# Eight rows for q and k, a permuted key order in PSUM, and a constant column for 1e-9 in a forgetting-attention and SwiGLU kernel

## The chip, the cores and the metric

The kernel runs on one core of one Trainium2 chip. The metric is device time in microseconds, and the median of three runs is the number that counts. The engines are named as in the profile: PE (TensorE, the matrix engine; PEld is its weight load), DVE (VectorE), ACT (ScalarE), POOL (GpSimd) and SP (SyncE, which here only issues DMAs). SBUF is the on-chip memory with 128 partitions, and PSUM is the small memory into which TensorE writes.

## The reference

Attention with a forget gate per position, then a SwiGLU feed-forward block over the heads put side by side. All inputs are float32.

```python
B, H, S, D = 8, 8, 576, 64
scores = (1 / sqrt(D)) * q @ k.T                       # per batch and head
cum    = cumsum(log(clip(f, 1e-4, 1)), axis=-1)
decay  = cum[..., :, None] - cum[..., None, :]
scores = where(causal, -1e9, scores + decay)           # causal: strictly above the diagonal
scores = scores - max(scores)
attn   = exp(scores)
attn   = attn / (sum(attn) + 1e-9)
x      = (attn @ v), heads side by side                # 4608 tokens x 512
g      = x @ w_gate                                    # 512 x 1536
out    = (g * sigmoid(g) * (x @ w_val)) @ w_out        # 1536 x 512
```

The term of the row in `decay` is the same for a whole row and cancels in the softmax, so only the column's `cum` matters.

## The kernel before, in words

**The planner.** The kernel lists some thousand operations, each with the engines that may run it, a price in ns on each, what it reads and writes, and a priority. A greedy list scheduler, `Plan.order` (L54), walks through them: it picks the operation and engine that can start first by those prices, gives it a buffer out of its pool, and so fixes the order on every engine. The buffers of a pool go out in a fixed turn. Each engine then runs its list in order. A changed price therefore changes the order of everything behind it. `SPARE` (L205) is a handicap that keeps some operations off ACT and DVE unless these are clearly earlier.

**The attention.** Work goes by pairs of heads: 32 pairs, four per batch (`p`). A pair's 576 queries are nine blocks of 64; a block of both heads fills the 128 output partitions. Blocks 0 to 3 are group 0 and blocks 4 to 8 group 1. For a pair:

- `load_pair` (L319) loads q and k with SP's queue: k as 96 partitions of 6 rows, q as 72 partitions of 8 rows (`ROWS`, L182). It also loads `cb`, the cumulated gates, spread over the partitions.
- `prepare` (L336) casts both to bfloat16 (L345 to L351; POOL, in the start also ACT or DVE) and transposes them on TensorE into a PSUM bank (L363): six transposes of 96 columns for k, eight of 72 for q. In the bank the positions then stand in the order (row within the partition, partition). The copy out of PSUM (L377 on ACT, L379 on DVE) reads them one by one in the order of the sequence: one copy of 128 partitions into `kt`, and two of 64 partitions into `qz`, which holds each head's queries in its own half, with zeros in the other.
- `scores` (L384) multiplies a block's queries with its keys (L398) and adds the mask of the diagonal block with an identity as weights (L402), with scores in PSUM with a minus sign. One DVE instruction (L414) then adds `cb` into `t` and takes the minimum of each row, and ACT takes the exponential with that minimum as bias and sums each row into `ls` (L428).
- `normalize` (L434) adds 1e-9 to `ls` in place (L437) and takes the reciprocal (L439), both on DVE; POOL (in the first eight pairs also ACT) multiplies the rows and packs them into `pk` as bfloat16 (L456). The packed weights are transposed by TensorE in the first eight pairs (L480, copied out at L485), and by DMA later.
- `weighted` multiplies with v (L506) and `spread` copies the result into `xT` (L530 on DVE or ACT), which feeds the feed-forward part.

**The feed-forward part.** Tiles of 256 or 512 tokens; per unit `gate` (L572) does the two products (L587), tanh on ACT into `th` (L593), and two DVE products (L595, L598) into `hh`; `project` multiplies with `w_out` (L612). Three PSUM banks (`gv`) serve the two products and the transposes. The feed-forward part of earlier tokens is threaded in between the attention of later ones; after about 345 us it is alone.

**The start.** The gates are clipped, taken the logarithm of, and cumulated by a DVE scan (L302), whose first input is a tile of ones.

Of the kernel before, what the change touches and what calls it, by code (L numbers as in the profile page):

```python
# [14 lines left out]
BIG = 1.0e9  # L15
# [142 lines left out]
def kernel(  # L158
# [23 lines left out]
    ROWS = {"k": (96, 6), "q": (72, 8)}  # L182
    scale = 1.0 / (D ** 0.5)
    assert NB * QB == S and D == 64 and all(a * b == S for a, b in ROWS.values())
# [39 lines left out]
    ident = sb.tile([P, P], BF16)  # L224
    maskf = sb.tile([P, QB], F32)
# [6 lines left out]

    bufs("qf", [P, 2, ROWS["q"][1] * D], F32, 2)
    bufs("kf", [P, 2, ROWS["k"][1] * D], F32, 2)
    bufs("qb", [P, ROWS["q"][1], 2, D], BF16, 2)
    bufs("kb", [P, ROWS["k"][1], 2, D], BF16, 2)
# [8 lines left out]
    bufs("ls", [P, NB], F32, 6)  # L245
# [5 lines left out]
    bufs("th", [P, 512], F32, 3)  # L251
# [10 lines left out]
    for h in range(2):  # L262
        nc.gpsimd.affine_select(
            out=maskf[64 * h:64 * h + 64, :], in_=maskf[64 * h:64 * h + 64, :],
            compare_op=ALU.is_ge, fill=BIG, base=0, pattern=[[-1, QB]], channel_multiplier=1,
        )
# [7 lines left out]
    setup({"POOL": 200}, lambda e: nc.gpsimd.tensor_copy(mask, maskf), ["mask"], -150)  # L274
    for n, qz in enumerate(pl.pools["qz"]):
        setup({"DVE": 800, "POOL": 1100}, lambda e, qz=qz: (eng[e].memset(qz[0:64, :, 1, :], 0.0),
                                                            eng[e].memset(qz[64:128, :, 0, :], 0.0)),
              [("z", "qz", n)], -95 if n == 0 else first[n] - 1.5)
    for i in range(0, NB, 2):
        for n, e_ in enumerate(pl.pools[f"e{i}"]):  # L280
            setup({"POOL": 100}, lambda e, e_=e_, i=i: nc.gpsimd.memset(e_[:, QB * (i + 1):], 0.0),
                  [("z", f"e{i}", n)], -80 if i < 4 else 1)
# [5 lines left out]
    ones = sb.tile([P, S], F32)  # L288
    pl.op({"POOL": 520}, lambda e: nc.gpsimd.memset(ones, 1.0), (), ["ones"], -200)
# [4 lines left out]
    def gates(key, parts, np_, prio):  # L294
        x = lambda: pl.buf(key)[0:np_, :]
        for n, (a, z, src) in enumerate(parts):
            loads["f", key, n] = pl.op({"SP": 600}, lambda e, a=a, z=z, src=src: nc.sync.dma_start(out=pl.buf(key)[a:z, :], in_=src),
                                       (), [(key, 0)] + [key] * (n == 0), prio + n * .01, dma=500)
        pl.op({"DVE": 460}, lambda e: nc.vector.tensor_scalar(x(), x(), 1.0e-4, 1.0, op0=ALU.max, op1=ALU.min),
              [(key, 0)], [(key, 1)], prio, holds=[key])  # L300
        pl.op({"ACT": 690}, lambda e: nc.scalar.activation(x(), x(), AF.Ln), [(key, 1)], [(key, 2)], prio, holds=[key])
        pl.op({"DVE": 1350}, lambda e: nc.vector.tensor_tensor_scan(x(), ones[0:np_, :], x(), 0.0, ALU.mult, ALU.add),  # L302
              [(key, 2), "ones"], [(key, 3)], prio, holds=[key])
# [15 lines left out]
    def load_pair(p):  # L319
        b, hp = divmod(p, NPB)  # L320
        s = first[p]
        for name, src, pr in (("k", k, 0), ("q", q, .1)):
            pl.key((name + "f", p), name + "f")
            loads[name, p] = pl.op({"SP": 620} if p else {"ACT": 620}, lambda e, name=name, src=src: (nc.scalar if e == "ACT" else nc.sync).dma_start(
                out=pl.buf((name + "f", p))[0:ROWS[name][0], :, :],
                in_=src[b, 2 * hp:2 * hp + 2].rearrange("h (p r) d -> p h (r d)", r=ROWS[name][1])),
                (), [(name + "f", p)], (-99 + 3 * p if p < NPB else s) + pr, dma=1130 if name == "k" else 980, after=[sums[p - 3, 0 if p - 3 >= NPB else 1]] if p >= NPB else [])
        if p >= NDIRECT:
            pl.key(("cb", p), "cb")
            for h in range(2):  # L330
                loads["cb", p, h] = pl.op({"SP": 600}, lambda e, h=h: nc.sync.dma_start(
                    out=pl.buf(("cb", p))[64 * h:64 * h + 64, :],
                    in_=cum_dram[2 * p + h:2 * p + h + 1, :].to_broadcast((64, S))),
                    ["cum_dram"], [("cb", p), (("cb", p), 3)], -98.5 + 3 * p if p < NPB else s + .2, dma=560)

    def prepare(p):  # L336
        s = first[p]
        for name in ("k", "q"):
            fk, bk = (name + "f", p), (name + "b", p)
            KR, KC = ROWS[name]  # L340
            pl.key(bk, name + "b")

            def cast(e, name=name, fk=fk, bk=bk, KR=KR):
                src = pl.buf(fk)[0:KR, :, :].rearrange("p h (r d) -> p r h d", d=D)
                dst = pl.buf(bk)[0:KR, :, :, :]  # L345
                if e == "ACT":
                    nc.scalar.activation(dst, src, AF.Copy, scale=-scale if name == "q" else 1.0)
                elif name == "q":
                    eng[e].tensor_scalar(dst, src, -scale, 1.0, op0=ALU.mult, op1=ALU.mult)  # L349
                else:  # L350
                    eng[e].tensor_copy(dst, src)  # L351
            engs = {"POOL": 850}
            if p < NPB:
                engs = {"POOL": 850, "ACT": 850, "DVE": 500} if name == "k" else {"POOL": 1050, "ACT": 1050, "DVE": 680}
# [5 lines left out]
            def transpose(e, bk=bk, tk=tk, KR=KR, KC=KC):  # L360
                src = pl.buf(bk).rearrange("p r h d -> p r (h d)")
                for j in range(KC):
                    nc.tensor.transpose(half(tk)[:, KR * j:KR * j + KR], src[0:KR, j, :], ident[0:KR, 0:KR])  # L363
            pl.op({"PE": KC * (KR / 2.4 + 2.5)}, transpose, [bk], [tk], s - 1, lat=200)
# [3 lines left out]
            for a, z, h in halves:  # L368
                def evac(e, a=a, z=z, h=h, tk=tk, ok=ok, KC=KC):
                    if h is None:  # L370
                        src = half(tk)[a:z, 0:S].rearrange("r (j p) -> r p j", j=KC)
                        dst = pl.buf(ok)[a:z, :].rearrange("r (p j) -> r p j", j=KC)
                    else:
                        src = half(tk)[a:z, 0:S].rearrange("r (j i p) -> r i p j", j=KC, i=NB)
                        dst = pl.buf(ok)[a:z, :, h, :].rearrange("r i (p j) -> r i p j", j=KC)
                    if e == "ACT":
                        nc.scalar.copy(dst, src)  # L377
                    else:
                        nc.vector.tensor_copy(dst, src)  # L379
                pl.op({"ACT": 600, "DVE": 680}, evac, [tk] + ([("z", "qz", p)] if h is not None and p < 5 else []), [ok], s - .9)  # L380
# [4 lines left out]
    def scores(p, g):  # L385
# [3 lines left out]
        for n, bank in enumerate(BANKS[g]):  # L389
# [4 lines left out]
            def mult(e, bank=bank, sk=sk):  # L394
                sp, kt, qz, o = pl.buf(sk), pl.buf(("kt", p)), pl.buf(("qz", p)), 0
                for i, a, z in bank:
                    last = z == QB * (i + 1)
                    nc.tensor.matmul(sp[:, o:o + z - a], qz[:, i, :, :].rearrange("p h r -> p (h r)"), kt[:, a:z],  # L398
                                     start=True, stop=not last)
                    o += z - a  # L400
                    if last:
                        nc.tensor.matmul(sp[:, o - QB:o], ident, mask, start=False, stop=True)  # L402
            cols = [z - a for _, a, z in bank] + [64 for i, a, z in bank if z == QB * (i + 1)]
            pl.op({"PE": mm(*cols)}, mult, [("kt", p), ("qz", p), "mask"], [sk], pr, lat=220)
            o = 0
            for i, a, z in bank:
# [5 lines left out]
                def add(e, i=i, a=a, z=z, o=o, sk=sk, tk=tk, last=last):  # L412
                    tm = pl.buf(("tm", p, g))
                    nc.vector.tensor_tensor_reduce(  # L414
                        out=pl.buf(tk)[:, a:z], in0=pl.buf(sk)[:, o:o + z - a], in1=pl.buf(("cb", p))[:, a:z], scale=1.0,
# [6 lines left out]
                if last:  # L422
# [3 lines left out]
                    def exp(e, i=i, tk=tk, ek=ek):  # L426
# [3 lines left out]
                                             accum_out=pl.buf(("ls", p, g))[:, i:i + 1])  # L430
# [3 lines left out]
    def normalize(p, g):  # L434
        s = at[p, g]
        ls = lambda: pl.buf(("ls", p, g))[:, LO[g]:HI[g] + 1]
        pl.op({"DVE": 90}, lambda e: nc.vector.tensor_scalar(ls(), ls(), 1.0e-9, None, op0=ALU.add),  # L437
              [("ls", p, g)], [("l1", p, g)], s, lat=120)
        pl.op({"DVE": 95}, lambda e: nc.vector.reciprocal(ls(), ls()), [("l1", p, g), ("ls", p, g)], [("l2", p, g)], s, lat=100)  # L439
# [3 lines left out]
        for i in range(HI[g], LO[g] - 1, -1):  # L443
            m = i // 2 + 1
            parts = [(0, m)] if (g, i) != (1, 8) else [(0, 4), (4, 5)]
            for c0, c1 in parts:
                def norm(e, i=i, c0=c0, c1=c1):
# [4 lines left out]
                    r = pl.buf(("ls", p, g))[:, i:i + 1]  # L452
# [6 lines left out]
                if p < FREE:  # L459
                    engs["ACT"] = L * .833 + 150  # L460
                o = pl.op(engs, norm,
                      [("e", p, i), ("l2", p, g), ("ls", p, g)] + [("z", f"e{i}", n) for n in range(2) if p == 0 and i % 2 == 0],
# [50 lines left out]
    def spread(p, g):  # L513
# [5 lines left out]
        for a, z in ((0, cut), (cut, w)):  # L519
# [3 lines left out]
            def evac(e, a=a, z=z):  # L523
                x0 = (t0 + a * QB) % NRING
                dst = xT[:, hp, x0:x0 + QB * (z - a)].rearrange("p (i r) -> p i r", r=QB)
                x = w - z
                src = pl.buf(xk)[:, QB * x:QB * (x + z - a)].rearrange("p (i r) -> p i r", r=QB)
                full = [list(d) for d in src.ap]
                src = bass.AP(src.tensor, src.offset + QB * (z - a - 1), [full[0], [-QB, z - a], full[2]])
# [181 lines left out]
```

## Time and profile before

| | |
|---|---|
| median of 3 runs | 439.18 us (438.22 to 440.01) |
| profiled execution | 437.54 us, span 435.8 us, mean granted TensorE clock 0.99 |
| PE busy | 405.7 us (93%) |
| DVE busy | 354.0 us (81%) |
| ACT busy | 296.7 us (68%) |
| POOL busy | 250.3 us (57%) |

The costliest groups of DVE, ACT and POOL (busy us, mean ns of one) that the change touches:

| line, engine | what | count | busy | mean |
|---|---|---|---|---|
| L414 DVE | subtraction and row minimum, all widths | 288 + 32 | 138.9 | |
| L379 DVE | copies of `kt` and `qz` out of PSUM | 53 | 39.7 | 750 |
| L377 ACT | the same on ACT | 43 | 27.0 | 627 |
| L351 POOL | cast of k | 31 | 25.4 | 821 |
| L349 POOL | cast of q | 31 | 33.0 | 1063 |
| L437 DVE | the addition of 1e-9 | 64 | 18.9 | 295 |
| L439 DVE | the reciprocal | 64 | 11.3 | 176 |
| L530 DVE, ACT | copy of the result into `xT` | 64 | 26.7 | |

The profile shows one execution. "Busy" is the time in which an engine had an instruction at work; matmuls are pipelined, so that a matmul's own duration (379 ns for 512 columns) is longer than the distance of two starts (216 ns). The chain of waits is the path of work that ended last, followed back from the end. A time on an engine matters where that engine is on this path or holds up one that is.

### The profile page before, as it was taken

The page shows a single profiled execution, that of the slowest core. Times are in us where ns is not written, and L with a number is a line of the kernel's source. Part 1 is how long each engine was busy: PE and PEld are TensorE (multiplying, and loading weights), DVE is VectorE, ACT ScalarE, POOL GpSimd, SP SyncE. Part 2 cuts the span into 40 slices and gives each one's busy share as a digit, 9 for nine tenths or more (in the row PEclk, how much of TensorE's full clock was granted, in tenths as well). Part 3 has the DMA queues.
Part 4 walks back from the last instruction along what each step waited for, and adds up shares of the span by engine and source line. Part 5 has one row for each costly group of instructions (what it writes and reads, how often), then busy time and mean ns, then how long its engine had stood idle before and what let it go on. Part 6 is the DMA issues. An engine that isn't in the chain of part 4 may idle for free.

```text
span 435.8 us, 9810 instructions
## 1 busy us (share of the span) xinstructions
PE 405.7 (93%) x3192; PEld 231.6 (53%) x3192; DVE 354.0 (81%) x1109; ACT 296.7 (68%) x824; POOL 250.3 (57%) x443
## 2 busy tenths in 40 slices
PE   2588999998899899999999999999999999999996
PEld 1445877755355455554554555555555444457672
DVE  7788799779999889999999999899999665365340
ACT  6887899979669767987766778787777633232321
POOL 6679828738957867787568677838973600000000
PEclk9996999999999999999999999999999999999999
DMA  7999899547869999999999999999984740010111
GB/s 201 213 193 233 173 204 212 149 125 202 191 149 221 218 224 207 203 231 217 219 204 228 208 206 222 201 197 218 208 160 99 119 106 26 24 50 24 50 50 72
DMA packets 143955, 72.50 MB, mean 166 GB/s; under 512 B 118560, under 2 KB 130592, under 8 KB 143904
## 3 DMA queue, kind: packets, MB, share of 16 engines
q1 hardware_dynamic: 137732, 66.57, 71.2%
q0 software_dynamic: 5808, 4.72, 7.3%
q10 hardware_dynamic: 364, 0.59, 0.5%
q8 instruction: 25, 0.41, 0.4%
q14 instruction: 26, 0.21, 0.2%
HBM read 47.33 MB, written 9.58 MB: 131 GB/s over the span
## 4 chain that ended last, share of the span: by engine, by line
PE 71%; DVE 13%; ACT 7%; issue 3%; DMA 2%; POOL 2%; SPq 1%; DVEq 0%; ACTq 0%
PE gv L587 35%; PE op L612 15%; PE sp L398 8%; PE tx L506 5%; DVE t L414 4%; PE tx L363 3%; ACT e L428 2%; PE gv L480 2%; PE gv L612 2%; ACT qz L377 2%; DVE qz L379 2%; DVE hh L598 2%; DMA qf<-in_q_dram 2%; DVE th L595 1%; ACT eo L428 1%
## 5 line engine op out<-in xcount | busy, mean ns | idle before, releaser
L414 DVE CUSTOM_DVE_ANT_0 t<-sp,cb 128x512 f32<-128x512 f32 (+7 forms) x288 | 130.2, 473 | 6.9 <-PE sp L402 3.1
L456 POOL TENSOR_SCALAR pk<-e,ls 128x128 bf16<-128x128 f32 (+3 forms) x184 | 98.1, 537 | 58.4 <-DVE tm L414 21.2
L587 PE MATMUL gv<-xT,wg 128*128 128x512 bf16 (+1 forms) x528 | 112.0, 342 | 0.0
L587 PE MATMUL gv<-xT,wv 128*128 128x512 bf16 (+1 forms) x528 | 111.2, 340 | 0.0
L428 ACT ACTIVATE e<-t,tm 128x448 f32<-128x448 f32 (+4 forms) x160 | 88.5, 554 | 26.4 <-DVE tm L414 26.0
L595 DVE SCALAR_TENSOR_TENSOR th<-th,gv 128x512 f32<-128x512 f32 x108 | 73.7, 683 | 37.4 <-ACT th L593 37.0
L593 ACT ACTIVATE th<-gv 128x512 f32<-128x512 f32 x108 | 63.7, 590 | 58.0 <-PE gv L587 57.1
L612 PE MATMUL op<-wo,hh 128*128 128x512 bf16 x396 | 100.6, 379 | 1.5 <-DVE ot L624 1.4
L398 PE MATMUL sp<-kt,qz 128*128 128x448 bf16 (+4 forms) x320 | 75.1, 301 | 10.2 <-DVE tm L414 8.5
L598 DVE TENSOR_TENSOR hh<-th,gv 128x512 bf16<-128x512 f32 x108 | 73.0, 683 | 9.2 <-PE op L612 3.8
L428 ACT ACTIVATE eo<-t,tm 128x256 f32<-128x256 f32 (+3 forms) x128 | 70.8, 553 | 4.0 <-DVE tm L414 2.9
L587 PEld LDWEIGHTS <-wg 128*128 128x128 bf16 x528 | 49.0, 99 | 36.6 <-issue 0.4
L587 PEld LDWEIGHTS <-wv 128*128 128x128 bf16 x528 | 48.3, 98 | 35.8
L456 POOL TENSOR_SCALAR pk<-eo,ls 128x128 bf16<-128x128 f32 (+3 forms) x121 | 64.7, 535 | 4.1 <-issue 1.6
L612 PEld LDWEIGHTS <-hh 128*128 128x128 bf16 x432 | 39.4, 98 | 40.6 <-issue 2.3
L402 PE MATMUL sp<-mask,ident 128*128 128x64 bf16 x288 | 48.8, 199 | 0.0
L398 PEld LDWEIGHTS <-qz 128*128 128x128 bf16 x320 | 31.0, 101 | 25.3 <-DVE qz L379 3.2
L402 PEld LDWEIGHTS <-ident 128*128 128x128 bf16 x288 | 27.5, 101 | 21.7 <-issue 11.6
L351 POOL CAST kb<-kf 96x768 bf16<-96x768 f32 x31 | 25.4, 821 | 20.1 <-DMA kf<-in_k_dram 15.1
L349 POOL TENSOR_SCALAR qb<-qf 72x1024 bf16<-72x1024 f32 x31 | 33.0, 1063 | 3.7 <-PE tx L363 1.5
L506 PE MATMUL tx<-pT,vt 128*64 128x320 bf16 (+4 forms) x448 | 30.0, 268 | 1.1 <-ACT qz L377 0.4
L428 ACT ACTIVATION_READ_ACCUMULATOR e<-t,tm 128x1 f32 x160 | 30.3, 190 | 0.0
(60 smaller groups left out, 396.2 us busy)
## 6 DMA issues: line engine op xcount, KB each, us to landing
out_dram<-ot SPq DMA_DIRECT2D x35, 256.0 KB
kf<-in_k_dram SPq DMA_DIRECT2D x31, 288.0 KB
qf<-in_q_dram SPq DMA_DIRECT2D x31, 288.0 KB
cb<-cum_f SPq DMA_DIRECT2D x62, 144.0 KB
vf<-in_v_dram SPq DMA_DIRECT2D x32, 256.0 KB
wo<-in_moe_w_out_dram POOLq DMA_DIRECT2D x3, 512.0 KB, 10.0
vf<-in_v_dram SPq DMA_DIRECT2D x8, 128.0 KB
wg<-in_moe_w_gate_dram POOLq DMA_DIRECT2D x2, 512.0 KB, 9.8
```

The costliest lines, as they stand in the source:

```text
L349: eng[e].tensor_scalar(dst, src, -scale, 1.0, op0=ALU.mult, op1=ALU.mult)
L398: nc.tensor.matmul(sp[:, o:o + z - a], qz[:, i, :, :].rearrange("p h r -> p (h r)"), kt[:, a:z], start=True, stop=not last)
L402: nc.tensor.matmul(sp[:, o - QB:o], ident, mask, start=False, stop=True)
L414: nc.vector.tensor_tensor_reduce(out=pl.buf(tk)[:, a:z], in0=pl.buf(sk)[:, o:o + z - a], in1=pl.buf(("cb", p))[:, a:z], scale=1.0, scalar= ...
L428: nc.scalar.activation(pl.buf(ek)[:, :L], pl.buf(tk)[:, :L], AF.Exp, bias=pl.buf(("tm", p, g))[:, i:i + 1], scale=-1.0, accum_out=pl.buf(( ...
L456: eng[e].tensor_scalar(dst, src, r, 1.0, op0=ALU.mult, op1=ALU.mult)
L506: nc.tensor.matmul(xo[r, 0:QB * n], vt[:, c, 2 * hp + h, :], pT[:, a:a + n, 64 * h:64 * h + 64], start=(c == 0), stop=(c == nch - 1))
L587: nc.tensor.matmul(pl.buf(bk)[:, j * n:j * n + n], wt[:, ko, fc * P:fc * P + P], xT[:, ko, x0:x0 + n], start=ko == 0, stop=ko == KD - 1)
L593: pl.op({"ACT": 487}, lambda e, u=u: nc.scalar.activation(pl.buf(("th", t, u)), pl.buf(("wg", t, u)), AF.Tanh, scale=0.5), [("wg", t, u)], ...
L595: pl.op({"DVE": 605}, lambda e, u=u: nc.vector.scalar_tensor_tensor(pl.buf(("th", t, u)), pl.buf(("th", t, u)), 1.0, pl.buf(("wg", t, u)), ...
L598: pl.op({"DVE": 605}, lambda e, u=u: nc.vector.tensor_mul(pl.buf(("hh", t, u)), pl.buf(("th", t, u)), pl.buf(("wv", t, u))), [("u", t, u), ...
L612: nc.tensor.matmul(pl.buf(bk), hh[:, (fc % nf) * n + ms * P:(fc % nf) * n + ms * P + P], wo[:, fc, :], start=fc == 0, stop=fc == KF - 1)
```

## The change

- **q and k by 8 rows.** Both are loaded as 72 partitions of 8 rows, cast, and transposed in eight steps of 72 columns. The tiles of k grow to 8 rows.
- **Copied from PSUM in runs.** `kt` is copied straight, in the order (row, partition), and `qz` in runs of eight partitions. Keys and the queries within a block of 64 thus stay in a permuted order.
- **The subtraction puts keys in order.** The score matmuls read `kt` in runs, so the scores' columns stand as (row, partition); L414 reads PSUM with a step and writes `t` in the order of the sequence. The mask's rows are permuted in its definition and by `perm`, a permuted identity, in place of `ident`; its product is added into runs of eight columns.
- **The copy of x puts queries in order.** `spread` writes `xT` with a step of eight elements.
- **1e-9 through a constant column.** `ls` gets a second column that holds 1e-9 (six memsets on POOL); a reduction over the two (DVE), or an addition (ACT), writes a new tile `lr`, and the reciprocal works on that.
- **The scan's ones** are one element of `tiny`, broadcast; the tile `ones` and its memset go. `th` has 2 buffers in place of 3.
- **Prices.** The cast is priced 1050 on POOL for both, the copies out of PSUM at 380 on DVE (680 before; ACT's 600 stays), the new addition at 95 on DVE and 200 on ACT.

```diff
-    ROWS = {"k": (96, 6), "q": (72, 8)}
+    R = 8
+    PR = S // R
...
+    perm = sb.tile([P, P], BF16)
...
-    bufs("ls", [P, NB], F32, 6)
+    bufs("ls", [P, NB, 2], F32, 6)
+    bufs("lr", [P, NB], F32, 6)
...
-    bufs("th", [P, 512], F32, 3)
+    bufs("th", [P, 512], F32, 2)
...
-            compare_op=ALU.is_ge, fill=BIG, base=0, pattern=[[-1, QB]], channel_multiplier=1,
+            compare_op=ALU.is_ge, fill=BIG, base=0, pattern=[[-1, R], [-R, R]], channel_multiplier=1,
...
+    setup({"POOL": 250}, lambda e: nc.gpsimd.tensor_copy(perm.rearrange("k (h j p) -> k h j p", h=2, j=R),
+                                                         ident.rearrange("k (h p j) -> k h j p", h=2, j=R)), ["perm"], -149)
...
+    for n, ls in enumerate(pl.pools["ls"]):
+        setup({"POOL": 120}, lambda e, ls=ls: nc.gpsimd.memset(ls[:, :, 1], 1.0e-9), [("z", "ls", n)], -70 if n < 2 else 0.5)
...
-        pl.op({"DVE": 1350}, lambda e: nc.vector.tensor_tensor_scan(x(), ones[0:np_, :], x(), 0.0, ALU.mult, ALU.add),
+        pl.op({"DVE": 1350}, lambda e: nc.vector.tensor_tensor_scan(x(), tiny[0:np_, 0:1].to_broadcast((np_, S)), x(), 0.0, ALU.mult, ALU.add),
...
-            engs = {"POOL": 850}
+            engs = {"POOL": 1050}
             if p < NPB:
-                engs = {"POOL": 850, "ACT": 850, "DVE": 500} if name == "k" else {"POOL": 1050, "ACT": 1050, "DVE": 680}
+                engs = {"POOL": 1050, "ACT": 1050, "DVE": 680}
...
                     if h is None:
-                        src = half(tk)[a:z, 0:S].rearrange("r (j p) -> r p j", j=KC)
-                        dst = pl.buf(ok)[a:z, :].rearrange("r (p j) -> r p j", j=KC)
+                        dst = pl.buf(ok)[a:z, :]
                     else:
-                        src = half(tk)[a:z, 0:S].rearrange("r (j i p) -> r i p j", j=KC, i=NB)
-                        dst = pl.buf(ok)[a:z, :, h, :].rearrange("r i (p j) -> r i p j", j=KC)
+                        src = src.rearrange("r (j i p) -> r i j p", j=R, p=R)
+                        dst = pl.buf(ok)[a:z, :, h, :].rearrange("r i (j p) -> r i j p", j=R)
...
-                pl.op({"ACT": 600, "DVE": 680}, evac, [tk] + ([("z", "qz", p)] if h is not None and p < 5 else []), [ok], s - .9)
+                pl.op({"ACT": 600, "DVE": 380}, evac, [tk] + ([("z", "qz", p)] if h is not None and p < 5 else []), [ok], s - .9)
...
-                    nc.tensor.matmul(sp[:, o:o + z - a], qz[:, i, :, :].rearrange("p h r -> p (h r)"), kt[:, a:z],
-                                     start=True, stop=not last)
+                    to = sp[:, o:o + z - a].rearrange("r (j p) -> r j p", j=R)
+                    nc.tensor.matmul(to, qz[:, i, :, :].rearrange("p h r -> p (h r)"),
+                                     kt.rearrange("d (j p) -> d j p", j=R)[:, :, a // R:z // R], start=True, stop=not last)
...
-                        nc.tensor.matmul(sp[:, o - QB:o], ident, mask, start=False, stop=True)
+                        nc.tensor.matmul(to[:, :, (z - a - QB) // R:], perm, mask.rearrange("r (j p) -> r j p", j=R),
+                                         start=False, stop=True)
...
-                        out=pl.buf(tk)[:, a:z], in0=pl.buf(sk)[:, o:o + z - a], in1=pl.buf(("cb", p))[:, a:z], scale=1.0,
+                        out=pl.buf(tk)[:, a:z].rearrange("r (p j) -> r p j", j=R),
+                        in0=pl.buf(sk)[:, o:o + z - a].rearrange("r (j p) -> r p j", j=R),
+                        in1=pl.buf(("cb", p))[:, a:z].rearrange("r (p j) -> r p j", j=R), scale=1.0,
...
-        pl.op({"DVE": 90}, lambda e: nc.vector.tensor_scalar(ls(), ls(), 1.0e-9, None, op0=ALU.add),
-              [("ls", p, g)], [("l1", p, g)], s, lat=120)
+        def guard(e):
+            if e == "ACT":
+                nc.scalar.add(lr(), ls()[:, :, 0], 1.0e-9)
+            else:
+                nc.vector.tensor_reduce(lr(), ls(), axis=mybir.AxisListType.X, op=ALU.add)
+        pl.op({"DVE": 95, "ACT": 200}, guard, [("ls", p, g)] + ([("z", "ls", n) for n in range(6)] if p < 3 else []), [("lr", p, g)], s, lat=120)
...
-                dst = xT[:, hp, x0:x0 + QB * (z - a)].rearrange("p (i r) -> p i r", r=QB)
+                dst = xT[:, hp, x0:x0 + QB * (z - a)].rearrange("d (i p j) -> d i j p", p=R, j=R)
...
-                src = bass.AP(src.tensor, src.offset + QB * (z - a - 1), [full[0], [-QB, z - a], full[2]])
+                src = bass.AP(src.tensor, src.offset + QB * (z - a - 1), [full[0], [-QB, z - a], [R, R], [1, R]])
```

## The prediction, before the run

> **What bounds the kernel now.** I read the page's first two parts, then the table of stages, then the chain of waits, then the timeline around the longest DVE piece of that chain, then the groups by shape.
>
> ```profile
> PE 405.7 (93%) x3192; PEld 231.6 (53%) x3192; DVE 354.0 (81%) x1109; ACT 296.7 (68%) x824; POOL 250.3 (57%) x443
> ...
> PEclk9996999999999999999999999999999999999999
> ```
>
> TensorE is busy for 93% of 435.8 us. One slice of forty, the fourth, shows a reduced granted clock. The stages say where the other 7% lies (columns: stretch, length, then PE, PEld, DVE, ACT and POOL busy, granted clock, DMA share, GB/s):
>
> ```profile
> 0.00:11.00 11.00, 2.73 (x28) 2.05 (x28) 7.81 (x15) 6.66 (x9) 7.02 (x27) 1.00 0.80 201
> 11.00:22.00 11.00, 6.30 (x66) 5.27 (x67) 8.25 (x35) 9.13 (x31) 7.50 (x10) 1.00 1.07 212
> 33.00:44.00 11.00, 9.52 (x71) 6.49 (x69) 9.11 (x34) 8.73 (x24) 10.90 (x19) 0.69 1.15 237
> 90.00:120.00 30.00, 26.42 (x227) 14.48 (x227) 28.35 (x100) 24.30 (x73) 21.71 (x39) 1.00 0.68 164
> 160.00:200.00 40.00, 39.47 (x316) 20.70 (x315) 39.32 (x132) 32.01 (x96) 29.03 (x52) 1.00 1.07 221
> 345.00:390.00 45.00, 45.00 (x231) 20.68 (x230) 23.06 (x36) 13.98 (x24) 3.07 (x7) 1.00 0.18 51
> ```
>
> From 160 us on TensorE is full, so time taken off another engine there buys nothing, and time added to TensorE is paid whole. What can be gained lies ahead of it: in the start, where DVE and ACT are 75 to 85% busy and TensorE idles for 13 of the first 22 us, and between 90 and 120 us, where DVE is 95% busy and TensorE idles 3.6 us. In the second of these the chain of waits (start, length, what) runs through DVE:
>
> ```profile
> 111.06 2.10 DVE ls L437
> ...
> 115.03 0.66 DVE qz L379
> 115.70 0.41 DVE ls L437
> ...
> 145.34 0.77 DVE qz L379
> ```
>
> L437 adds 1e-9 to five numbers per partition, and yet takes 2.1 us. The timeline shows why:
>
> ```profile
> 110.98 2.18 DVE L437 TENSOR_SCALAR ls<-ls 128x5 f32<-128x5 f32 x1
> ...
> 111.30 0.82 POOL L351 CAST kb<-kf 96x768 bf16<-96x768 f32 x1
> 112.09 1.04 POOL L349 TENSOR_SCALAR qb<-qf 72x1024 bf16<-72x1024 f32 x1
> ```
>
> It ends at 113.16, as POOL's run of casts ends at 113.13: DVE stands behind POOL. At 193.17 it takes 1.09 us beside a POOL cast that starts at 193.19 and takes 1.03.
>
> **The change part by part.** The rows for prices:
>
> ```profile
> L437 DVE TENSOR_SCALAR ls<-ls 128x5 f32<-128x5 f32 x32 | 9.8, 306 | 1.0 <-ACT e L428 1.0
> L439 DVE RECIPROCAL ls<-ls 128x5 f32<-128x5 f32 x32 | 5.8, 182 | 0.0
> L379 DVE COPY kt<-tx 128x576 bf16<-128x576 bf16 x21 | 15.8, 752 | 1.8 <-PE tx L363 1.3
> L485 DVE COPY pT<-gv 128x1024 bf16<-128x1024 bf16 x10 | 6.6, 681 | 1.8 <-PE tx L506 1.8
> L485 DVE COPY pT<-gv 128x384 bf16<-128x384 bf16 x4 | 1.4, 349 | 0.5 <-PE gv L480 0.5
> ```
>
> *The 1e-9.* The 64 additions take 18.9 us of DVE (9.8 above, 9.1 for the four-wide form); the undisturbed ones take 0.17. The reduction over a pair (sum, constant) that replaces them is not in the trace. The nearest row is the reciprocal, on the same numbers and beside the same POOL work: 182 and 171 ns, so 11.3 us for 64 and 7.6 us less. On the path: the pieces at 111.06 and 115.70 fall to 0.17, -2.2 us. If the reduction stood behind POOL as the addition does, this is 0; if the 1.01 us that the chain has at 193.25 also counted, -3.1. I take -2.2, since 64 reciprocals never stood behind POOL. The planner may also put it on ACT (it prices that at 200), where it delays the next exponential by about that.
>
> *k and q out of PSUM.* Today each of the 96 copies of 576 columns gathers single elements: 752 ns for kt and 747 for the qz halves on DVE, 1.04 ns per element above 150. The pT copies read runs and lie on a line of 0.52 ns per element, which gives 0.45 us at 576. DVE's 53 copies become 0.30 us shorter, 15.9 us in all. ACT's 43 stay: 0.63 gathered, against 0.64 from its own pT rows (478 at 384, 797 at 768). The planner's new DVE price (380 against ACT's 600) will move copies from ACT to DVE, so ACT is relieved too. On the path: DVE qz at 115.03, 145.34 and 154.60, -0.9; kt at 51.86 and qz at 52.79, -0.6; three ACT copies of 0.63 at 12.56, 13.21 and 17.61, -0.5 where DVE takes them at 0.45. That is -2.0. Ends: 0, if each is covered by the engine next in line, and -4.9, if all of the page's chain shrinks (DVE qz 1.6% of the span, or 7.0 us, by 0.30/0.75; ACT qz 1.7%, or 7.4 us, by 0.18/0.63).
>
> *k by 8 rows.* POOL's cast of k becomes the shape of q's: 821 to 1063 ns, 31 times, +7.5 us on POOL, which has 10 of 40 us free in the long middle. In the start two k casts stand in POOL's queue ahead of q casts that are on the chain: +0.4 (ends 0 and +0.7, three times 0.24). The first, on ACT, grows 0.2 us and is covered, since the chain there is the landing of the second pair's q (3.27 to 9.97 us). The load has the same 288 KB in 2 KB pieces instead of 1.5 KB, priced 0. Eight transposes of 72 columns in place of six of 96: the starts are 32 and 42 ns apart, 260 against 252 ns per pair, +0.2 us of TensorE.
>
> *The subtraction in another order.* 320 DVE instructions (138.9 us) now read PSUM in rows of eight single elements. That is how L379 reads today, at 1.04 ns per element, and L414 already costs that: 682 ns at 512, 274 at 128, 1.06 per element. So 0. The least sure of the zeros; its other end is a rival.
>
> *Output copy.* The 64 copies (13.4 us on DVE, 13.3 on ACT) now write SBUF in single elements 16 bytes apart; no row writes so. Low end 0, as gathered reading has no price beyond 1.04. High end: the 0.52 ns that runs save at L485, times 288 elements, 0.15 us each, +4.5 on DVE and +5.1 on ACT. I take half, and +0.3 on the path (two chain pieces at 30.29 and 33.42); ends 0 and +1.0.
>
> *Score and mask matmuls.* The keys are read in runs of 8 to 64, and the mask is added into runs of 8. L506 reads runs of 64 at full rate (320 columns, two halves side by side, every 135 ns). Taken 0; the other end is a rival.
>
> *th from 3 to 2.* Of 106 cases, the tanh two units on starts over 0.4 us after the product that frees its buffer in 101. In the five others (217, 260, 306, 347, 380 us) that product waits for TensorE's projection; the next unit's product, 0.68 us, then covers the tanh of 0.59. 0; without that cover 5 x 0.6 = +3.0.
>
> *Setup on POOL.* A memset of 0.58 leaves, a permuted copy (the mask's cast took 0.24) and six memsets of about 0.1 come; POOL idles 2.5 us before its first cast at 8.71. 0.
>
> Sum: -2.2 - 2.0 + 0.4 + 0.2 + 0.3 = -3.3 us. The profiled execution took 437.54 (span 435.8 and 1.7 around it), so 434.2; the runs' median is 1.64 above it, so I forecast 435.9.
>
> **Rivals.**
>
> *TensorE pays for short runs (slower).* Behind each of the 288 mask matmuls the next starts 29 ns later; writing scattered runs they could hold it twice that long, the factor between L379 and L485. It decides as soon as one exceeds 29 ns, since TensorE is full: +8.4 us, so 444.3. Against it: the run is still eight elements, and the score output stays contiguous. "PSUM — Partial Sum Buffer" (Specifications) of the Trainium skill speaks for it: PSUM has 8-byte lines, and any pattern that is not contiguous is said to slow matmuls significantly. No run here shows it yet.
>
> *The subtraction pays for its gather (much slower).* At +0.52 ns on 2880 x 32 elements DVE gets +48 us. It is 89 to 98% busy from 90 to 330, so what the 23 us of relief leaves, some +25, is paid: about 464. L379's rows speak against it. The Trainium skill, "Vector Engine (DVE) Microarchitecture Reference" (5.2), has 1.73 ns per element against 1.05 where one of two sources hops every element, and 1.71 for a hopping destination; by it DVE would get +63 us. It was measured between SBUF regions, and L379's PSUM reads don't follow it.
>
> *The relief is covered (no change).* TensorE is full after 160 us, the start hangs on a landing, and the list order is drawn anew: 437 to 441.
>
> *The new order loses.* From 90 to 160 us POOL has seven more k casts' growth to bear (1.7 us) and DVE and ACT 14 output copies (2.1), and POOL already carries the chain for 4.6 us from 97.95. If nothing covers them, +3.8 us on a relief that went elsewhere: 443.0.
>
> *A denser start.* At 0.69 of the clock over 11 us TensorE loses 3.4 us there. Fewer gaps before could spare it: 432.5.
>
> **How the numbers follow.** Forecast 0.32; denser start 0.14; covered 0.22; TensorE pays 0.15; new order loses 0.10; subtraction pays 0.07. Faster by over 0.5% (2.2 us, about what a measurement of this kernel can tell from no change): 0.46; within: 0.22; slower: 0.32. The likeliest case alone gives 431.2 (best ends, -8.0) to 437.0. The range: down to -8.0 and half of the 3.4, 429.5; up to the matmul rival with the copies worth nothing and k cast and output copy at their worst, -2.2 + 0.7 + 1.0 + 0.2 + 8.4 = +8.1, 447.3. The subtraction's case is left out.
>
> **What would show it.** The DVE copies at 0.45; the reductions at 0.18 with none over 0.3; the 512-wide subtraction at 0.68; 64-column mask matmuls 29 ns from the next start; TensorE idle below 3 us between 90 and 120. A subtraction at 0.9 or mask matmuls 50 ns apart would make me wrong.

## The result: 4.3% slower, and the profile after

The changed kernel takes 458.1 us (median of 4 runs, 457.11 to 459.63) against 439.6 us before: a ratio of 1.043 (95% interval 1.038 to 1.048), or +18.5 us. The forecast was 435.9, and 458.1 lies outside its range. The profiled execution took 457.57 us (span 455.8).

The page's first two parts answer to the lines shown of before:

```profile
PE 409.2 (90%) x3256; PEld 231.1 (51%) x3256; DVE 364.0 (80%) x1089; ACT 323.6 (71%) x841; POOL 257.5 (56%) x452
...
PEclk9997999999999999999999999999999999999999
```

DVE has 10.0 us more work instead of less, ACT 26.9 us more. The granted clock is the same. The table of stages (columns as before):

```profile
33.00:44.00 11.00, 9.11 (x71) 5.56 (x71) 9.46 (x33) 8.38 (x24) 10.95 (x19) 0.69 1.10 222
90.00:120.00 30.00, 26.86 (x254) 15.15 (x251) 26.98 (x89) 26.38 (x75) 20.82 (x35) 1.00 0.67 163
160.00:200.00 40.00, 37.39 (x291) 19.21 (x291) 36.23 (x115) 30.82 (x82) 26.80 (x46) 1.00 0.98 200
...
345.00:390.00 45.00, 43.06 (x261) 20.56 (x260) 33.00 (x82) 25.52 (x60) 13.73 (x27) 1.00 0.42 79
```

From 160 to 200 us TensorE was busy for 39.47 of 40 us before and is now for 37.39: it waits where it was full. The stretch from 90 to 120, where the forecast saw its gain, still idles 3.1 us. The chain of waits names what is in the way (shares by engine before; then by engine and by line after):

```profile
PE 71%; DVE 13%; ACT 7%; issue 3%; DMA 2%; POOL 2%; SPq 1%; DVEq 0%; ACTq 0%
```

```profile
PE 43%; DVE 27%; ACT 17%; issue 7%; DMA 4%; SPq 1%; POOL 1%; DVEq 0%; ACTq 0%; POOLq 0%
PE gv L605 20%; PE op L630 12%; DVE t L423 10%; DVE xT L548 5%; ACT e L439 5%; DVE th L613 4%; DMA qf<-in_q_dram 4%; ACT xT L548 4%; DVE hh L616 4%; ACT eo L439 4%; PE sp L406 3%; PE tx L370 2%; PE tx L524 2%; ACT th L611 2%; PE gv L630 2%
```

The copy of x, L548, has 9% of the span on the chain. Pieces of 0.9 to 1.65 us stand there all along, for instance (start, length, what):

```profile
169.16 1.50 DVE xT L548
...
179.78 1.65 ACT xT L548
...
190.55 1.50 DVE xT L548
```

The groups show how much it grew (busy us, mean ns of one). First two shapes of this copy before, where it stands in L530; then the page's lines of all 64 after:

```profile
L530 ACT CAST xT<-tx 128x320 bf16<-128x320 f32 x19 | 7.9, 416 | 6.2 <-PE tx L506 6.0
...
L530 DVE CAST xT<-tx 128x320 bf16<-128x320 f32 x13 | 6.3, 487 | 2.5 <-PE tx L506 2.5
```

```profile
L548 DVE CAST xT<-tx 128x320 bf16<-128x320 f32 (+1 forms) x32 | 46.1, 1451 | 6.3 <-PE tx L524 6.1
L548 ACT CAST xT<-tx 128x256 bf16<-128x256 f32 (+1 forms) x32 | 45.1, 1442 | 6.2 <-PE tx L524 6.1
```

Added up by shape, the 64 copies took 26.7 us before and take 92.5 now (91.2 by the lines above, which count overlap once). The other changed steps are close to their forecasts; the groups by shape:

```profile
L423 DVE CUSTOM_DVE_ANT_0 t<-sp,cb 128x512 f32<-128x512 f32 x64 | 45.2, 706 | 2.8 <-ACT lr L453 0.7 <-PE sp L406 0.7 <-ACT ot L640 0.6
...
L358 POOL CAST kb<-kf 72x1024 bf16<-72x1024 f32 x31 | 31.9, 1031 | 13.8 <-DMA kf<-in_k_dram 12.9 <-PE sp L410 0.9
...
L386 DVE COPY kt<-tx 128x576 bf16<-128x576 bf16 x19 | 8.6, 455 | 3.3 <-PE tx L370 2.7 <-ACT e L439 0.5
...
L455 DVE TENSOR_REDUCE lr<-ls 128x5 f32<-128x10 f32 x23 | 3.9, 170 | 0.9 <-ACT e L439 0.5 <-issue 0.3
```

The copies in runs take 0.455 us (forecast 0.45) and the reductions 0.17 (0.18); 31 of the 64 additions went to ACT. Two of the 33 reductions took 0.377 us, each starting in the tail of a scattered copy on its own engine. The 512-wide subtraction, with its columns gathered from PSUM, has a mean of 706 ns and a median of 687, against a mean of 682 before. The gather isn't what lengthens it: with the same gather and x written straight (the first experiment) its mean is 683, and with the subtraction of before and x scattered (the second) 710.

### The profile page after: what moved, and what is told of

The parts are those of the page before. It is cut to its first block, busy times and chain, and to the rows that moved or that the text cites. A ratio compares the mean times of both kernels' runs of the same rounds, so it can differ in the third digit from the quotient of the medians.

```text
span 455.8 us, 9986 instructions
## 1 busy us (share of the span) xinstructions
PE 409.2 (90%) x3256; PEld 231.1 (51%) x3256; DVE 364.0 (80%) x1089; ACT 323.6 (71%) x841; POOL 257.5 (56%) x452
## 4 chain that ended last, share of the span: by engine, by line
PE 43%; DVE 27%; ACT 17%; issue 7%; DMA 4%; SPq 1%; POOL 1%; DVEq 0%; ACTq 0%; POOLq 0%
PE gv L605 20%; PE op L630 12%; DVE t L423 10%; DVE xT L548 5%; ACT e L439 5%; DVE th L613 4%; DMA qf<-in_q_dram 4%; ACT xT L548 4%; DVE hh L616 4%; ACT eo L439 4%; PE sp L406 3%; PE tx L370 2%; PE tx L524 2%; ACT th L611 2%; PE gv L630 2%
## 5 line engine op out<-in xcount | busy, mean ns | idle before, releaser
L423 DVE CUSTOM_DVE_ANT_0 t<-sp,cb 128x512 f32<-128x512 f32 (+7 forms) x288 | 133.6, 487 | 8.0 <-PE sp L410 4.4
L474 POOL TENSOR_SCALAR pk<-e,lr 128x512 bf16<-128x512 f32 (+3 forms) x186 | 97.6, 528 | 67.9 <-DVE lr L457 29.5
L439 ACT ACTIVATE e<-t,tm 128x448 f32<-128x448 f32 (+4 forms) x160 | 90.3, 566 | 22.4 <-DVE tm L423 22.3
L439 ACT ACTIVATE eo<-t,tm 128x256 f32<-128x256 f32 (+3 forms) x128 | 73.0, 571 | 9.6 <-DVE tm L423 6.4
L474 POOL TENSOR_SCALAR pk<-eo,lr 128x512 bf16<-128x512 f32 (+3 forms) x122 | 64.6, 529 | 4.5 <-DVE lr L457 2.9
L548 DVE CAST xT<-tx 128x320 bf16<-128x320 f32 (+1 forms) x32 | 46.1, 1451 | 6.3 <-PE tx L524 6.1
L548 ACT CAST xT<-tx 128x256 bf16<-128x256 f32 (+1 forms) x32 | 45.1, 1442 | 6.2 <-PE tx L524 6.1
L410 PE MATMUL sp<-mask,perm 128*128 128x64 bf16 x288 | 48.2, 198 | 0.0
L406 PEld LDWEIGHTS <-qz 128*128 128x128 bf16 x320 | 31.0, 101 | 26.7 <-DVE qz L386 4.8
L410 PEld LDWEIGHTS <-perm 128*128 128x128 bf16 x288 | 27.0, 100 | 27.6 <-issue 18.3
L358 POOL CAST kb<-kf 72x1024 bf16<-72x1024 f32 x31 | 31.9, 1031 | 13.8 <-DMA kf<-in_k_dram 12.9
```

The source lines that it names most:

```text
L406: nc.tensor.matmul(to, qz[:, i, :, :].rearrange("p h r -> p (h r)"), kt.rearrange("d (j p) -> d j p", j=R)[:, :, a // R:z // R], start=Tru ...
L410: nc.tensor.matmul(to[:, :, (z - a - QB) // R:], perm, mask.rearrange("r (j p) -> r j p", j=R), start=False, stop=True)
L423: nc.vector.tensor_tensor_reduce(out=pl.buf(tk)[:, a:z].rearrange("r (p j) -> r p j", j=R), in0=pl.buf(sk)[:, o:o + z - a].rearrange("r (j ...
L439: nc.scalar.activation(pl.buf(ek)[:, :L], pl.buf(tk)[:, :L], AF.Exp, bias=pl.buf(("tm", p, g))[:, i:i + 1], scale=-1.0, accum_out=pl.buf(( ...
L474: eng[e].tensor_scalar(dst, src, r, 1.0, op0=ALU.mult, op1=ALU.mult)
L548: (nc.scalar.copy if e == "ACT" else nc.vector.tensor_copy)(dst, src)
```

## Experiments

Theory A: writing x one 2-byte element at a time costs several times what was taken, holds DVE and ACT, and through them the two `tx` banks. Theory B: the copy is a symptom, and the order redrawn by the new prices, the cast of k or the smaller `th` is what costs. Ratios are to runs of the kernel before on the same chip.

### The copy of x

**Read with a step, write straight.** The only edit to the changed kernel:

```diff
-  dst = xT[...].rearrange("d (i p j) -> d i j p", p=R, j=R);  src = AP(..., [R, R], [1, R]])
+  dst = xT[...].rearrange("d (i p j) -> d i p j", p=R, j=R);  src = AP(..., [1, R], [R, R]])
```

> The changed kernel, but the copy of x reads PSUM with a step and writes xT in runs, as the subtraction does, in place of reading runs and writing with a step. Theory (the scattered write is the whole loss): the 64 copies of x fall from 1.3 to 1.6 us back to 0.36 to 0.49 us, DVE and ACT lose some 64 us of work together, and the time is 435 to 437 us, a little below the kernel before. Rival (the loss is in the new order, the third tanh buffer that is gone, or the gathering subtraction): the copies get short but the time stays above 448 us.

Measured: 445.7 us, ratio 1.014 (1.009 to 1.020), between the two forecasts. The same 64 copies, read in steps from PSUM, cost about what they did before the change (487 ns on DVE and 416 on ACT for 320 columns):

```profile
L548 DVE CAST xT<-tx 128x320 bf16<-128x320 f32 x17 | 8.3, 487 | 2.2 <-PE tx L524 1.9
...
L548 ACT CAST xT<-tx 128x320 bf16<-128x320 f32 x15 | 6.3, 419 | 6.9 <-PE tx L524 6.7
...
L423 DVE CUSTOM_DVE_ANT_0 t<-sp,cb 128x512 f32<-128x512 f32 x64 | 43.7, 683 | 5.8 <-PE sp L406 2.1 <-PE sp L410 1.6 <-ACT lr L453 1.5
```

12.4 of the 18.5 us are this one pattern; some 6 us are something else.

**The scattered write alone**, in the kernel before (this lets the queries of a block come out in another order):

```diff
-  dst = xT[...].rearrange("p (i r) -> p i r", r=QB);  src = AP(..., full[2]])
+  dst = xT[...].rearrange("d (i p j) -> d i j p", p=8, j=8);  src = AP(..., [8, 8], [1, 8]])
```

> The kernel before, with one edit: the copy of x writes xT with a step of eight elements (so the tokens within a block of 64 come out in another order; nothing else differs, and the planner's prices and order are those of before). Theory: the 64 copies take 1.3 to 1.6 us, and the time rises by 15 to 22 us, to 455 to 462 us. Rival (the scattered write is mostly covered, and the loss is elsewhere in the change): it rises by less than 6 us.

Measured: 464.6 us, ratio 1.060 (1.056 to 1.065), +25 us. The pattern alone costs more than the whole change does, and more than its forecast of 15 to 22 us. No price, order or size was touched, so theory A holds for it. Since DVE, ACT and POOL run the same instructions in the same order as before, the two traces can be laid side by side: the lag is 5.9 us at 97 us, 8.1 at 150, 13.0 at 196 and 26.9 at 345. Some 19 of the 27 us between these two executions arise from 150 to 345 us.

**The planner told the truth.** The changed kernel with the copy's price at what the trace shows (ACT `3.95*n+310`, DVE `4.27*n+215`):

> The changed kernel with the planner told what the scattered copy of x really costs (3.95 ns per element and 310 on ACT, 4.27 and 215 on DVE, from the rows of the changed kernel, in place of 0.83 and 130, 1.04 and 85). The instructions are the same, only order and engines may differ. If the loss is the time that the copies hold engines and the bank they read, the plan recovers at most a third: 452 to 458 us. If it is that a plan with wrong prices makes engines wait for one another in the wrong order, most of it comes back: 438 to 446 us.

Measured: 450.1 us, ratio 1.027 (1.023 to 1.032). Neither end: 8.0 us of the 18.5 come back with every copy as slow as before (1575 and 1585 ns for 320 columns). So part of the loss lies in the order, which had been drawn up with a price nearly four times too low. How much of the 8.0 is the truth of the price isn't shown, since any new price draws another order, and one such change below moved the time by some 5 us.

**The price of a write by its pattern**, measured by itself, without the attention, in one execution:

> No attention at all: copies of 320 elements out of PSUM (and two out of SBUF), each form six times on DVE and on ACT, then ACT's scattered copy beside straight DVE copies into another tile. What makes the scattered write slow? If it is each element's new 16-byte line: single bf16 elements at steps of 16 and 64 bytes cost over 4 ns each, steps of 4 and 8 bytes half or less, and float32 elements 16 bytes apart as much as bf16 ones. If it is the write of 2 bytes alone (a partial word): every single bf16 element costs over 4 ns whatever its step, pairs (4 bytes) cost 1 ns, and float32 at any step costs 1 ns. If it is coming back to the same line eight times: only the form of the change costs 4 ns, and steps without return cost about 1. Gathered reads from PSUM cost 1.04 ns on DVE and 0.83 on ACT in all of these. Beside ACT's scattered copies, DVE's straight copies of 512 stay at 0.68 us, or grow by some 0.2 us if the two share a write path.

Copies of 320 elements from PSUM; the groups by shape are, in this order, the change's form, single 2-byte elements 4 and 8 bytes apart, pairs of them 16 bytes apart, 4-byte words in the change's form, and the gathering read with a straight write:

```profile
L56 DVE CAST db<-src 128x320 bf16<-128x320 f32 x6 | 9.3, 1557 | 0.2
...
L57 DVE CAST db<-src 128x320 bf16<-128x320 f32 x6 | 3.1, 514 | 0.2
...
L58 DVE CAST db<-src 128x320 bf16<-128x320 f32 x6 | 5.2, 866 | 0.2
...
L61 DVE CAST db<-src 128x320 bf16<-128x320 f32 x6 | 3.0, 492 | 0.2
...
L65 DVE COPY df<-src 128x320 f32<-128x320 f32 x6 | 4.4, 728 | 0.2
...
L68 DVE CAST db<-src 128x320 bf16<-128x320 f32 x6 | 2.9, 480 | 0.0
```

ACT takes 1559, 514, 866, 439, 730 and 427. A straight copy takes 481 and 426; elements 16 bytes apart that never come back to the same stretch still take 1572, and at 64 bytes 1545. Above a fixed 0.15 us, a lone 2-byte element costs 4.4 ns at 16 bytes and more, 2.2 at 8 bytes and 1.1 at 4, on both engines; a pair costs next to nothing extra. A gathering read from PSUM is free, and one from SBUF takes 725 ns on DVE, against 326 straight. None of the three forecasts holds as put: 4-byte words 16 bytes apart cost less than half as much (718 ns), the distance matters, and coming back doesn't. The price is measured; why a lone 2-byte element costs it stays open.

### The other 6 us

**Each small part alone, in the kernel before.** The constant column with its reduction:

> The kernel before with the 1e-9 through a constant column (reduction or ACT's addition into lr) and the scan's ones from one element, nothing else. My prediction's term for it is -2.2 us (ends 0 and -3.1): 436 to 439.5 us, no reduction above 0.3 us where the addition had 2.18. Rival: ACT's additions stand in front of exponentials and the reciprocal moves onto the packing's path: 441 us or more.

437.7 us, ratio 1.000 (0.997 to 1.003). `th` with 2 buffers:

> The kernel before with th in 2 buffers in place of 3, nothing else. My prediction put this at 0 (at most +3.0): 439 to 440 us. Rival: the third buffer mattered, since a tanh that waits holds a PSUM bank that the transposes and gates share: 442 us or more, and then it is part of what keeps x_gather behind.

439.1 us, ratio 1.004 (1.001 to 1.007). k by 8 rows, with `th` at 2 and the cast's new price:

> The kernel before with k by 72 partitions of 8 rows (load, cast, eight transposes, gathered copy, prices as in the change), and, to make room, th with 2 buffers and the scan's ones from one element. Nothing else of the change. If k by 8 rows is what costs x_gather its 6 us (POOL +7.5 us, or later landings), 444 to 448 us; if not, 438 to 441.

448.5 us, ratio 1.023 (1.019 to 1.028). That is more than what was left to explain. Then the casts of k moved off POOL to DVE, in the version that reads x with a step:

> The kernel with x copied by gathering (445.7 us), and k's cast given to DVE (price 680) in place of POOL. In that kernel the chain from 160 us on runs through POOL (packing 14% of it, cast of q 3%) and landings of k, v and the transposed weights. If POOL's extra 7.5 us of k casts is what keeps it 6 us behind the kernel before, POOL falls by 32 us, DVE rises by some 20 to 357, and the time is 434 to 439 us. If the DMA landings or the order are the cause, it stays at 443 to 448.

507.4 us, ratio 1.160, far outside both forecasts. POOL lost 22 us of work, but the order was drawn anew, and POOL's cast of q then waited for TensorE's transposes, in six waits of up to 13.2 us (waited for: total us, times, longest):

```profile
POOL qb L356 <- PE tx L370: 62.5, 6, 13.2
```

The granted clock was lower too, 0.93 on average against 0.99, and 0.85 to 0.93 in the stages from 120 to 390 us. So this run says little about POOL's casts.

**Order or instructions?** k by 8 rows with all prices as before, so that each engine's list is that of `th` at 2 alone, but for two more transposes per pair; and the new price of the cast alone (`{"POOL": 850}` to 1050, and the start's accordingly), with no instruction changed:

> The kernel before with k loaded, cast and transposed in 72 partitions of 8 rows, th with 2 buffers (the tile of k leaves no room for 3), the scan's ones one broadcast element, and all of the planner's prices as before, so that every engine's order is the same as with th at 2 buffers alone (which took 439.1 us). The k copies still read PSUM one by one. Theory A, the redrawn order is what k by 8 rows costs: 438 to 441. Theory B, the instructions themselves (a POOL cast 0.24 us longer 31 times, a load that lands later): 445 to 450, as when the order was redrawn too (448.5).

> The kernel before with one price of the planner changed: the cast of k at 1050 on POOL and ACT and 680 on DVE, in place of 850 and 500. No instruction changes, only their order. Theory A, the redrawn order: 443 to 450. Theory B, the instructions: 437 to 441.

447.9 us, ratio 1.021 (1.017 to 1.024), and 442.7 us, ratio 1.011 (1.007 to 1.015). The instructions, in an unchanged order, cost 1.7 points more than `th` alone, some 7 us. The price alone costs some 5 us through the order it draws, just below theory A's range; but 1050 is the price of a cast of 1024 elements, and this kernel still casts 768 in 0.83 us, so here it is wrong. Where it is right, the order it draws costs nothing that can be seen: k by 8 rows took 448.5 us (1.023) with it and 447.9 (1.021) without. Since the order is equal in `th` at 2 alone and in k by 8 rows with the old prices, the two traces can be laid side by side instruction by instruction: the lag is 0.3 us at 97, 1.7 at 196, 5.3 at 250 and 9.6 at 327 us. It grows where POOL waits for loads, in steps of 1.5 to 3 us at 214, 231, 298, 309 and 321 us. The waits of POOL with `th` at 2 alone, and then with k by 8 rows in the same order:

```profile
POOL kb L351 <- DMA kf<-in_k_dram: 16.4, 12, 5.9
POOL vt L549 <- DMA vf<-in_v_dram: 15.2, 16, 2.1
```

```profile
POOL vt L549 <- DMA vf<-in_v_dram: 25.3, 17, 5.1
POOL kb L351 <- DMA kf<-in_k_dram: 19.7, 9, 8.3
```

**The number of DMA engines?** The trace has a packet of 4 bytes for each engine that completes a load; with k by 8 rows there are 4568 of them in place of 4692, four fewer for each of 31 loads. So the load of k in 96 partitions ends on 16 DMA engines and one in 72 on 12, and by division each carries 24 KB in place of 18. "DMA: Bandwidth & Descriptors" of the Trainium skill ("Why a DMA increments its semaphore by 16 and not by 1") has the rule: the largest number up to 16 that divides the slowest dimension of both sides. The completions agree. Whether it costs was tried by splitting loads, with orders and casts unchanged: k's 96 partitions as 72 + 24 (12 engines) and as 64 + 32 (16), k by 8 rows as 64 + 8, and q, which always had 72, as 64 + 8.

```diff
+  for lo, hi in ((0, 72), (72, 96)):   # or (0, 64), (64, 96)
+      nc.sync.dma_start(out=kf[lo:hi, :, :], in_=x[lo:hi, :, :])
```

> The kernel before, its order and casts unchanged; each load of k (96 partitions of 6 rows) goes as two transfers, of 72 and 24 partitions. By the completions in the trace both run on 12 DMA engines, 24 KB on each, as a load in 72 partitions of 8 rows does. If the 12 engines are what k by 8 rows costs: 444 to 449, and at least 5 us above the split into 64 and 32. If POOL's casts are: 437 to 441, within 1.5 us of it.

> The control for the split into 72 and 24: the same with 64 and 32 partitions, both on 16 DMA engines, 18 KB on each, as in the kernel before. It carries the same 32 more DMA issues on the queue of SP. 438 to 441 by both theories, unless the additional issues cost by themselves.

> k by 8 rows in the order of before (447.9 us), with each load of k as two transfers, of 64 partitions (16 engines) and 8 (8 engines): the busiest DMA engine carries 20 KB in place of 24. If the engines are the cause, four sixths of the 9 us come back: 441 to 443, plus what the control shows for the additional issues. If POOL's casts: 447 to 449.

> The kernel before with the load of q (72 partitions of 8 rows, on 12 DMA engines, 24 KB on each) as two transfers of 64 and 8 partitions: 20 KB on the busiest. If the busiest engines set the pace from 150 us on: 431 to 436. If they do so only with k's larger share: 438 to 440. If the issues on SP cost: above 440.

Measured: 440.3 (ratio 1.008), 443.8 (1.013), 449.4 (1.026) and 439.1 us (1.003). The second, the control, was forecast at 438 to 441 and missed. Of the two splits of k before, which carry the same issues, the one on twelve engines did no worse than the one on sixteen, and spreading q brought nothing. That speaks against the engines theory. The split of k by 8 rows decides nothing: the two splits of k before cost 3 to 6 us by themselves, and 441 to 443 plus that reaches 449.

**POOL's casts, or the load?** A repeated part of the cast behind each cast of k in the kernel before; k by 8 rows with the cast, and with the load, cut to 6 of the 8 rows from the fifth pair on:

```diff
+  eng[e].tensor_copy(dst[:, 0:1, :, 0:48], src[:, 0:1, :, 0:48])        # POOL only
...
+  eng[e].tensor_copy(dst[:, 0:6], src[:, 0:6])                          # cast cut
...
+  out=kf[0:72, :, 0:384], in_=...[:, :, 0:384]                          # load cut
```

> The kernel before in its own order; behind each cast of k on POOL a second one repeats 96 of its elements, which by the two casts' slope (0.86 ns per element and 0.16) adds some 0.25 us, as the 72 x 1024 cast does. If POOL's time is what k by 8 rows costs: 444 to 449. If not: 437 to 440.

> k by 8 rows in the order of before (447.9 us), but from the fifth pair on the cast covers 6 of the 8 rows (the other two keep an older pair's values), so that it takes the 0.82 us of before. If POOL's time is the cost: 438 to 442. If the load is: 446 to 449.

> k by 8 rows in the order of before, but from the fifth pair on the load brings 6 of the 8 rows (1.5 KB per partition and head in place of 2 KB; the rest keeps an older pair's values), with the full cast. If the load's bytes are the cost: 438 to 442. If POOL's time: 446 to 449. If both matter, each kernel gives back a part.

Measured: 440.5 (ratio 1.002, 0.998 to 1.005), 447.4 (1.016, 1.012 to 1.020) and 443.7 us (1.009, 1.006 to 1.013). The added casts were there:

```profile
L351 POOL CAST kb<-kf 96x96 bf16<-96x96 f32 x31 | 9.2, 296 | 1.9
```

9.2 us more of POOL did nothing that can be told from noise, and taking the growth away gave back some 2 us, which lies within the intervals. Taking a quarter off the load gave back 5, and POOL's waits for k and v fell from 45.0 to 26.0 us (7.8 and 18.2; 31.6 with `th` at 2 alone). The two other steps of k take as long with 8 rows as with 6: the copies of `kt` take 752 ns on DVE and 624 and 625 on ACT, and the transposes 14.4 and 14.5 us in all. So the load is what is left. But the lighter load carries less than the one before the change (216 KB against 288), so the run shows that the transfers weigh here, not why 288 KB in 72 partitions are slower than in 96.

**A version with q alone in runs**, k left at 96 by 6, x read with a step, the mask through a permuted identity:

> The kernel before with q alone copied out of PSUM in runs (priced 400 on DVE), so that a block's queries stand in another order; a permuted identity for the mask, and x read from PSUM with a step and written straight. k, th and the addition of 1e-9 are as before. If the shorter copies are worth what the prediction gave them on the path (two thirds of 2.0 us): 435 to 438. If they are covered: 438 to 441. If a redrawn order alone costs up to 10 us: above 443.

446.6 us, ratio 1.018 (1.013 to 1.023). The qz copies on DVE did fall to 453 ns, and TensorE from 160 to 200 us still fell to 37.30 busy us. No version tried beats the kernel before.

## Why the prediction was wrong, point by point

- **Output copy: the term that failed.** It was priced at +0.15 us each at most, half of it taken, +0.3 on the path. Measured +1.0 us each, some 65 in all; alone it cost 25 us, and undoing it gave back 12.4 of the 18.5. The high end came from L485, what runs save on the reading side in PSUM; that row says nothing of writing to SBUF, no row did, and nothing kept the cost below it. The Trainium skill's figure for a hopping destination, quoted in the rival on the subtraction, was weighed against the wrong instruction. "Vector Engine (DVE) Microarchitecture Reference" (5.2) of the Trainium skill gives 1.71 ns per element against 1.05; laid on the output copy, (1.71 - 1.05) x 288, it would have been an estimate of 0.19 us each. The 4-byte words above come close to it (728 ns for 320, so 1.8 ns each above 0.15 us); the 2-byte ones cost 2.4 times as much. The list of what would show a mistake didn't watch this copy: the two signs named, a subtraction at 0.9 and mask matmuls 50 ns apart, both stayed away.
- **TensorE is full after 160 us.** From this the prediction took that a gain of another engine buys nothing there, and it counted the output copy only by two pieces of the chain at 30 and 33 us. That doesn't hold for a loss: some 19 of the 27 us of the scattered write alone arose from 150 to 345 us. The same line of the stages had DVE at 39.32 of 40 us, so there was hardly any cover for 1 us more per copy. Two slips changed nothing: for the start, "75 to 85% busy" misreads the rows (DVE has 71 and 75%, ACT 61 and 83%), and the best end of -8.0 leaves out the 0.2 us of the transposes.
- **k by 8 rows: +0.4, measured some +7** in an unchanged order. By elimination it was the pricing of the load at nothing that failed, not that of the casts. The stages had shown the 16 DMA engines with a mean share of 1.07 from 160 to 200 us, and nothing was read from it. Engines as full as that leave no room to call a changed load free.
- **The 1e-9: -2.2, measured 0.** The reductions didn't stand behind POOL, as forecast (154 and 159 ns in the run with this part alone, 168 at most), so the low end of 0 came true without the reason given for it. Whether other engines covered the gain, as the third rival had it, or the new order took it, no run separates.
- **Copies in runs: -2.0.** Their duration was right. Alone, for q, they brought no gain but a loss of 1.8%. That the order that came with them lost it is likely, but no run had the shorter copies in the old order.
- **th at 2: 0, measured +1.7 us.** The end of +3.0 held it.
- **The new order loses: 443.0, chance 0.10.** That the price of k's cast alone gave 442.7 is chance: the rival was made of longer casts on POOL and longer output copies, and that run has neither. Its two parts came out apart: 9.2 us of casts cost nothing, and the copies cost much more than its 2.1 us. A redrawn order by itself had been priced only in the third rival, at 441 at most.
- **Right:** the subtraction's free gather, TensorE's indifference to runs of 8 (a mask matmul is still followed 28 to 29 ns later, against what "PSUM — Partial Sum Buffer" (Specifications) of the Trainium skill says of patterns that are not contiguous), and the durations of casts, reductions and copies out of PSUM, but for that of x.

What stays open: why k's load by 8 rows makes the transfers late, and how the parts add. The two traces in the same order give a hint on the first: packets of 1.5 and 2 KB (k, q and the output) took 93.2 us per DMA engine (the mean of 16) with `th` at 2 alone and 92.8 with k by 8 rows, but the 256-byte ones, those of v among them, 181 and 192. So it may not be k's own packets that take longer; with one execution each, that isn't shown. Alone they come to +25 for the scattered write, about +7 for k and +1.7 for `th`, together only +18.5; each redraws or delays the same schedule, and they overlap.

## What to carry to other kernels

When a permutation must be undone, undo it on the side that reads PSUM, and let the write to SBUF run straight; if a write must be scattered, keep whole 4-byte words or pairs together. A cost that no row shows has no upper bound from a row of another memory or direction: keep the rival open until one is measured. In a kernel whose order comes from prices, a wrong price can cost twice, once in time and once in the order, and a changed price can cost a per cent with no instruction changed.

## What the runs showed of the hardware

- A 2-byte element written to SBUF by itself, 16 bytes or more from the next, costs 4.4 ns on DVE and on ACT alike, 2.2 if its neighbour is 8 bytes away, 1.1 at 4 bytes; a lone 4-byte word costs 1.8 ns, and pairs and runs go at full rate.
- A gathering read from PSUM costs neither engine anything (480 and 427 ns against 481 and 426 straight); the same read from SBUF takes 725 and 763, against 326 and 457 straight.
- While ACT wrote lone 2-byte elements, DVE's straight copies of 512 kept their 690 ns (three of them ran wholly beside such writes, at 85, 88 and 89 us), so no shared limit shows.
- A load over 72 partitions completes on 12 DMA engines, one over 96 on 16.
